# Engine orders found by single-move search and written out, in a fused block-sorted attention and gated SSM kernel

## Chip, cores and metric

One core of a Trainium2 chip. The metric is the device time in microseconds (us) of one execution. Lower is better. Each comparison runs both kernels in turn on the same chip. The granted clock is the share of full speed that the trace records for TensorE. Executions in which it is low or the time stands apart are marked slow; comparisons are made between fast runs.

Names used below: PE is TensorE, ACT ScalarE, DVE VectorE, POOL GpSimd, SP SyncE. The profile calls the instruction streams of SP and POOL "SPq" and "POOLq".

## The reference

Attention over sequences that are cut into 8 blocks of 96, where keys and values are first mixed across blocks by a matrix P (five Sinkhorn rounds of row and column normalisation), and then a gated layer with a linear scan over the sequence:

```python
batch, n_heads, seq, head_dim = (4, 8, 768, 64)          # 8 blocks of 96
# P: five rounds of exp, row and column normalisation of sort_net
k_sorted = einsum('bhij,bhjcd->bhicd', P, k_b)            # v_sorted alike
attn = softmax(scale * q_b @ k_sb.T)                      # per block
x = (attn @ v_sb) ...                                     # -> (4, 768, 512)
proj = x @ w_in                                           # 512 -> 1024
val, gate = proj[..., :512], proj[..., 512:]
h = a[0, 0] * h + val[:, t, :]; ys[:, t, :] = h           # scan over t
out = (silu(gate) * ys) @ w_out                           # 512 -> 512
```

## The kernel before

The kernel does not write its instructions down in order. It declares some 780 operations with what each reads and writes, its possible engines and an assumed cost, and a list scheduler in the same file turns them into one order per engine while the kernel is built. Semaphores keep these orders on the chip: each engine takes its operations as they are written, so one late operand stops everything behind it on that engine.

Names of operations (`b` is the batch, `h` the head, `p` the pair of heads, 4 pairs to a batch):

- `ld_QB`, `ld_KB`, `ld_VB`, `ld_wout`: loads from HBM, issued by POOL. POOL also does the gate multiplications `um`.
- `vs b_h` (PE) and `vse b_h` (ACT or DVE): sorted V of one head, and its copy from PSUM, the memory that PE writes its products to, into the buffer VSS.
- `vm b`: the **move** of a whole batch's sorted V from VSS to VA, which brings it to another set of partitions. It is 8 DMAs issued by SP, and needs all eight `vse` of its batch.
- `av p_k` (PE): attention times V, the first reader of VA. `rz`, `xn` (DVE, some ACT) normalise it, `xt` (PE) transposes it.
- `ks`, `kse`, `qt`, `qte`: sorted K and transposed Q with their copies. `pv`, `pg` (PE): projections. `o`, `oe`: outputs.

```python
HW_DMA = {"store": (2000.0, 7300.0, 780.0), "move": (3000.0, 6700.0, 2600.0), ...}   # ns
...
if o.kind in ("load", "fine"):
    dma_free = max(dma_free, t + cost) + o.dma / LOAD_RATES[o.kind == "fine"]
    ...
else:
    now = t + cost                          # SP has issued all pieces
    quick, slow, moved = HW_DMA[o.kind]
    if dma_free > now:                      # loads placed so far are still in flight
        o.end = now + slow
        ...                                 # and those loads are made later
    else:
        o.end = max(now, hw_free) + quick
```

So a move is booked at 5.1 us of issue plus 6.7 us if the load queue, by this reckoning, still has work at the instant SP is done, and at 5.1 plus 3.0 if it has none. The choice is made once, when the move is placed. Loads issued after that are never held against it.

The order itself came from priorities, with a correction for each operation in a long hexadecimal string (the scheduler's inner loop is cut here; the form of a matmul is the part of PE's array that it uses, `128*128` or `128*64` in the lines below; in the chain of the kernel before, 24 matmuls of the second form take 0.79 us behind the first and 0.67 behind their own):

```python
key = max(t, t_min) + pull * o.prio         # smallest key goes next on its engine
if e == "PE" and o.mode != mode:
    key += stick * ENTER[o.mode]            # a change of form counts against it
...
P.schedule(8, pull=5.859375, stick=0.1, nudge=NUDGE)
```

The softmax here doesn't subtract the row's maximum and nothing guards it: scores larger than these inputs give would overflow.

## Time and profile before

| | before |
|---|---|
| time, median of 3 runs | 123.95 us (123.77 to 125.11) |
| profiled span | 121.7 us |
| first sorted-K product / first projection / PE's end | 12.74 / 27.62 / 118.57 us |
| granted clock, whole span | 1.00 |

The 27.62 is where the view of the chain starts the first projection, and the prediction uses it. PE's timeline has it at 27.46, which is the figure to set beside the timelines of the other kernels.

This is SP's timeline of the kernel before, with start, length, engine, line and operation of the three moves:

```profile
28.55 5.22 SPq L671 DMA_DIRECT2D VA<-VSS  x8
49.82 5.90 SPq L671 DMA_DIRECT2D VA<-VSS  x8
69.52 5.07 SPq L671 DMA_DIRECT2D VA<-VSS  x8
```

And this is PE's timeline at the first readers of the first two moves. A bracket at a line's end gives the idle time before it and what ended it:

```profile
40.34 0.51 PE L733 MATMUL PSA<-VA,EX 96*128 96x65 bf16 x11
...
62.13 0.36 PE L733 MATMUL PSA<-VA,EX 96*128 96x65 bf16 x6 [0.22 <-DMA VA<-VSS]
```

From the start of SP's issue to the first use, 11.8 and 12.3 us pass. PE does not wait at the first, and waits 0.22 us at the second, so both moves are hidden with nearly nothing to spare. By the view of DMA issues, one piece of the first two moves takes 6.0 and 6.1 us to land, and one of the third, when loads are over, takes 2.8.

### The profile page before, as it was taken

The page shows a single profiled execution, that of the slowest core. Times are in us where ns is not written, and L with a number is a line of the kernel's source. Part 1 is how long each engine was busy: PE and PEld are TensorE (multiplying, and loading weights), DVE is VectorE, ACT ScalarE, POOL GpSimd, SP SyncE. Part 2 cuts the span into 40 slices and gives each one's busy share as a digit, 9 for nine tenths or more (in the row PEclk, how much of TensorE's full clock was granted, in tenths as well). Part 3 has the DMA queues.
Part 4 walks back from the last instruction along what each step waited for, and adds up shares of the span by engine and source line. Part 5 has one row for each costly group of instructions (what it writes and reads, how often), then busy time and mean ns, then how long its engine had stood idle before and what let it go on. Part 6 is the DMA issues. An engine that isn't in the chain of part 4 may idle for free.

```text
span 121.7 us, 3684 instructions
## 1 busy us (share of the span) xinstructions
PE 112.2 (92%) x1485; PEld 74.7 (61%) x1485; DVE 100.0 (82%) x239; ACT 84.0 (69%) x183; POOL 59.5 (49%) x84
## 2 busy tenths in 40 slices
PE   1689989999999999999999999999799999999990
PEld 1577778765766777667556586766466655554530
DVE  3774897999998999977599999999799999995300
ACT  4126879999868988898866977887634423365761
POOL 7999999999955620200028065000011396235500
PEclk9999999999999999999999999999999999999999
DMA  1999999999999999999999868289892000422665
GB/s 6 149 176 188 199 212 209 204 205 203 217 247 236 202 208 215 225 251 239 253 293 251 128 102 154 100 151 144 287 260 48 5 0 0 172 89 86 226 252 216
DMA packets 26305, 21.33 MB, mean 175 GB/s; under 512 B 7472, under 2 KB 22832, under 8 KB 26288
## 3 DMA queue, kind: packets, MB, share of 16 engines
q0 software_dynamic: 13824, 11.01, 58.3%
q1 hardware_dynamic: 12464, 10.08, 30.8%
q8 instruction: 12, 0.20, 0.6%
q14 instruction: 5, 0.04, 0.1%
HBM read 22.03 MB, written 6.29 MB: 233 GB/s over the span
## 4 chain that ended last, share of the span: by engine, by line
PE 66%; DMA 10%; DVE 9%; ACT 4%; SPq 4%; POOL 2%; issue 1%; POOLq 0%
PE PSA L800 31%; PE PSA L836 14%; DMA VA<-VSS 6%; PE PSA L733 5%; DVE XN L754 5%; DMA QB<-in_q_dram 4%; SPq L671 4%; PE PSA L703 4%; PE PSA L609 4%; PE PSA L625 3%; PE PSA L662 2%; ACT EX L713 2%; PE PSA L776 1%; DVE XT L417 1%; DVE RZ L745 1%
## 5 line engine op out<-in xcount | busy, mean ns | idle before, releaser
L819 POOL TENSOR_TENSOR GA<-GA,YS 128x384 bf16<-128x384 bf16 x30 | 27.2, 917 | 55.3 <-DVE GA L816 32.0
L800 PE MATMUL PSA<-XT,WIN 128*128 128x384 bf16 x256 | 45.4, 326 | 0.8 <-DVE XN L754 0.8
L800 PEld LDWEIGHTS PSA<-XT,WIN 128*128 128x128 bf16 x256 | 23.9, 98 | 16.3 <-DVE XN L754 0.9
L713 ACT ACTIVATE EX<-PSA 96x384 bf16<-96x384 f32 x64 | 26.3, 488 | 2.4 <-PE PSA L703 2.1
L813 ACT ACTIVATE TH<-PSA 128x384 f32<-128x384 f32 x32 | 15.7, 492 | 15.0 <-PE PSA L800 13.8
L836 PE MATMUL PSA<-WOUT,GA 128*128 128x512 bf16 (+1 forms) x100 | 23.2, 370 | 0.0
L754 DVE TENSOR_TENSOR XN<-PSA,RZ 96x320 bf16<-96x320 f32 (+2 forms) x49 | 21.7, 470 | 0.2
L816 DVE SCALAR_TENSOR_TENSOR GA<-TH,PSA 128x384 bf16<-128x384 f32 x32 | 17.0, 542 | 5.3 <-ACT TH L813 4.2
L415 ACT ACTIVATE OUTSB<-PSA 128x512 f32<-128x512 f32 (+1 forms) x23 | 13.4, 581 | 7.3 <-PE PSA L836 7.1
L807 DVE TENSOR_TENSOR_SCAN YS<-AEXP,YS,PSA 128x384 bf16<-128x384 f32 x16 | 15.7, 999 | 0.3 <-PE PSA L800 0.2
L807 DVE TENSOR_TENSOR_SCAN YS<-AEXP,PSA 128x384 bf16<-128x384 f32 x16 | 14.8, 940 | 0.7 <-PE PSA L800 0.7
L733 PE MATMUL PSA<-VA,EX 96*128 96x65 bf16 x256 | 13.7, 194 | 0.5 <-DVE XN L754 0.2
L836 PEld LDWEIGHTS PSA<-WOUT,GA 128*128 128x128 bf16 x100 | 9.0, 97 | 8.2 <-ACT OUTSB L415 0.3
L733 PEld LDWEIGHTS PSA<-VA,EX 96*128 96x128 bf16 x256 | 10.9, 98 | 4.7 <-DMA VA<-VSS 0.8
L745 DVE RECIPROCAL RZ<-PSA 96x5 f32<-96x5 f32 (+2 forms) x52 | 8.3, 175 | 2.0 <-PE PSA L733 1.6
L415 ACT ACTIVATE KTS<-PSA 128x768 bf16<-128x768 f32 x11 | 8.6, 811 | 1.4 <-PE PSA L625 1.3
L703 PE MATMUL PSA<-QTS,KTS 64*96 64x96 bf16 x256 | 9.5, 210 | 0.0
L703 PEld LDWEIGHTS PSA<-QTS,KTS 64*96 64x96 bf16 x256 | 7.2, 121 | 3.6 <-DVE KTS L417 0.4
L609 PE MATMUL PSA<-IDENT,QB 128*64 128x128 bf16 x192 | 7.8, 238 | 1.3 <-DMA QB<-in_q_dram 1.3
L415 ACT ACTIVATE VSS<-PSA 128x384 bf16<-128x384 f32 x19 | 8.4, 504 | 0.3 <-PE PSA L662 0.3
L625 PE MATMUL PSA<-LALL,KB 128*64 128x128 bf16 x192 | 7.4, 221 | 0.7 <-ACT EX L713 0.6
L427 POOL DMA_DIRECT2D QB<-in_q_dram x10 | 7.7, 782 | 0.3 <-issue 0.3
(60 smaller groups left out, 122.2 us busy)
## 6 DMA issues: line engine op xcount, KB each, us to landing
out_dram<-OUTSB SPq DMA_DIRECT2D x23, 256.0 KB, 2.5
VA<-VSS SPq DMA_DIRECT2D x24, 97.5 KB, 5.7
VB<-in_v_dram POOLq DMA_DIRECT2D x6, 384.0 KB, 20.1
KB<-in_k_dram POOLq DMA_DIRECT2D x6, 384.0 KB, 23.9
QB<-in_q_dram POOLq DMA_DIRECT2D x6, 384.0 KB, 21.5
WIN<-in_moe_w_in_dram POOLq DMA_DIRECT2D x1, 1024.0 KB, 11.1
QB<-in_q_dram POOLq DMA_DIRECT2D x4, 192.0 KB, 5.1
KB<-in_k_dram POOLq DMA_DIRECT2D x4, 192.0 KB, 6.1
```

What stands on the lines that cost most here:

```text
L415: return eng.activation(dst, src, AF.Copy, scale=1.0 if scale is None else scale)
L609: ins = e.transpose(PSB[u.bank][64 * x:64 * x + 64, t * 128:(t + 1) * 128], QB[sl][:, 2 * pr + x, t * 64:(t + 1) * 64], IDENT[:, :])
L703: ins = e.matmul(PS[us[half, x].bank][0:BLK, il * BLK:(il + 1) * BLK], KTS[ks][r, i * BLK:(i + 1) * BLK], qt(r, i))
L713: op("ex%d_%d_%d" % (p, half, x), act_cost(HALF), lambda e, n, u=us[half, x], es=es, half=half: e.activation(EX[es][:, half, 0:HALF].rearr ...
L733: ins = e.matmul(PS[u.bank][:, (kk - k0) * 65:(kk - k0 + 1) * 65], EX[es][:, i // 4, (i % 4) * BLK:(i % 4) * BLK + 128], VA[vs][:, i, hx * ...
L754: return e.tensor_tensor(XN[xs][:, k0 * D:(k0 + nb) * D].rearrange("p (n d) -> p n d", d=D), pv(u, nb)[:, :, 0:64], bass.AP(RZ[rz], 0, [[6 ...
L800: ins = e.matmul(PS[u.bank][:, 0:HALF], WIN[:, c, col:col + 128], XT[(4 * b + c) % NXT][:, half * HALF:(half + 1) * HALF], start=(c == 0), ...
L807: op("sc%d_%d_%d" % (b, ch, half), {"DVE": 65 + 384 * 2.1}, lambda e, n, u=u: e.tensor_tensor_scan(YS[slot][:, :], AEXP[:, ch:ch + 1].to_b ...
L813: op("th%d_%d_%d" % (b, ch, half), act_cost(HALF), lambda e, n, u=w: e.activation(TH[ts][:, :], PS[u.bank][:, 0:HALF], AF.Tanh, scale=0.5) ...
L816: op("ga%d_%d_%d" % (b, ch, half), dve_cost(HALF), lambda e, n, u=w: e.scalar_tensor_tensor(GA[slot][:, :], TH[ts][:, :], 1.0, PS[u.bank][ ...
L819: op("um%d_%d_%d" % (b, ch, half), {"POOL": 900, "DVE": 500} if b == B - 1 and half else {"POOL": 900}, lambda e, n: e.tensor_tensor(GA[sl ...
L836: ins = e.matmul(PS[u.bank][:, 0:c1 - c0], GA[slots[ch]][:, tl * 128:(tl + 1) * 128], WOUT[:, ch, c0:c1], start=(ch == 0), stop=(ch == 3))
```

## The change

Intent: take the order that the scheduler had found, improve it by trying single moves of operations (and of copies between ACT and DVE), each judged by a timetable of the same kind that keeps the order fixed and also counts loads that come late, and write the best orders into the kernel. No operation is added or removed. 18 copies go from ACT to DVE and 18 back. POOL now issues the last loads between gate multiplications instead of ahead of all of them.

```diff
-NUDGE = ("787d6199da75884466907dde6a737596fd557b9f2b38bd7a8772678d756e7c8d..." (cut)
+ORDER = (
+    "004f0050005100aa005200670053005400550056007b005700580059005a005c..."   # PE (cut)
+    ...                                                    # ACT, DVE, POOL, SP
+)
-    def schedule(self, n_banks, pull=0.0, stick=1.0, nudge=None):
+    def replay(self, n_banks, order):
+        todo = {e: [self.ops[int(x[i:i + 4], 16)] for i in range(0, len(x), 4)] for e, x in zip(engines, order)}
... (choice by priority removed; the earliest head of the five orders is placed next)
+                if at[e] == len(todo[e]) or todo[e][at[e]].left:
                     continue
+                o = todo[e][at[e]]
+                t = max(o.ready, free[e])
... (PSUM banks by the same rule as before; the branch on dma_free is unchanged)
-        P.schedule(8, pull=5.859375, stick=0.1, nudge=NUDGE)
+        P.replay(8, ORDER)
```

## The prediction

> **What bounds the kernel now.** I read the page's busy shares first, then its chain of work, TensorE's waits, the busy time in five stretches, and last the merged chain, for unit costs.
>
> ```profile
> PE 112.2 (92%) x1485; PEld 74.7 (61%) x1485; DVE 100.0 (82%) x239; ACT 84.0 (69%) x183; POOL 59.5 (49%) x84
> ...
> PE 66%; DMA 10%; DVE 9%; ACT 4%; SPq 4%; POOL 2%; issue 1%; POOLq 0%
> ```
>
> TensorE (PE) is busy 92% of the span of 121.7 us and is two thirds of the chain; VectorE (DVE) follows at 82%. All that TensorE waited for, in the whole run:
>
> ```profile
> PE PSA L539 <- ACT PSA L517: 2.7, 1, 2.7
> PE PSA L609 <- DMA QB<-in_q_dram: 1.3, 2, 0.9
> PE PSA L800 <- DVE XN L754: 0.8, 1, 0.8
> PE PSA L625 <- ACT EX L713: 0.6, 1, 0.6
> PE PSA L554 <- DVE PT L548: 0.3, 1, 0.3
> PE PSA L733 <- DVE XN L754: 0.2, 1, 0.2
> PE PSA L733 <- DMA VA<-VSS: 0.2, 1, 0.2
> ```
>
> The first is the start. The two waits for Q loads (1.3) fall before 9 us, where the Sinkhorn steps on DVE and ScalarE (ACT) set the pace to 10.9 us anyway. After that only 2.1 us of named waits are left. The stretches, cut at the first sorted-K product (12.74), the first projection (27.62), the first attention product of batch 2 (62.13), the last projections, and TensorE's end (118.57):
>
> ```profile
> 12.74:27.62 14.88, 13.79 (x289) 10.96 (x290) 13.65 (x41) 14.09 (x34) 14.85 (x26) 1.00 1.25 206
> 27.62:62.13 34.51, 34.29 (x525) 22.84 (x523) 30.16 (x64) 29.60 (x69) 12.96 (x16) 1.00 1.26 230
> 62.13:101.69 39.56, 38.80 (x477) 25.11 (x478) 38.06 (x85) 25.25 (x54) 13.50 (x15) 1.00 0.66 139
> ```
>
> Columns: length, then busy time of PE, PEld, DVE, ACT, POOL, the clock, the DMA share, GB/s. In the first stretch DVE and ACT are as full as PE: it is bound by emptying PSUM. In the second, PE never visibly stops. In the third DVE is nearly as full as PE (38.1 to 38.8 of 39.6). Transfers run at a share over 1 until about 67 us: the queue of input loads is full for half the run.
>
> **What is hidden in "busy".** Four neighbouring rows of the merged chain (start, duration):
>
> ```profile
> 31.98 0.79 PE PSA L625 x24
> 32.77 0.67 PE PSA L609 x24
> 33.45 0.67 PE PSA L625 x24
> 34.12 4.01 PE PSA L800 x24
> ```
>
> The same 24 column-half matmuls take 0.79 us when they come after a full-array matmul and 0.67 after their own kind; 24 projection matmuls after them take 4.01, where 24 x 0.1625 (20 take 3.25 elsewhere in the chain) is 3.90. So each change of array form costs about 0.115 us. Other unit costs, from start to start in the same view: projection group of 4, 0.65; output group of 4, 0.865; 16 score matmuls 0.37 plus the change; one attention-value matmul 0.031; 12 sorted or Q-transpose matmuls 0.335; one V-sort matmul 0.163; 8 transposes 0.345.
>
> [...]
>
> **How much could be won.** Units times counts, from 12.74 to 118.57. First stretch: work 10.2, 15 changes of form 1.7, together 11.9 of 14.88: 3.0 us lost. Second: work 31.8 (21 projection groups 13.65, 6 outputs 5.2, 16 sorted or Q sets 5.4, the rest 7.6), 21 changes 2.4, together 34.2 of 34.51: 0.3 lost. Third, to the end: work 53.7 (43 projection groups 28.0, 18 outputs 15.6, the rest 10.1), 14 changes 1.6, together 55.3 of 56.44: 1.1 lost, 0.76 of it the one wait for DVE at 85.6. In all 4.4 us lost and 5.8 us of changes. No operation is added or removed, so these are all that a new order can attack; start and tail (2.5 us of the last copy and store after PE's end) stay. 2% is 2.5 us: more than half of all losses.
>
> **The change part by part.** I decoded both orders into names of operations. Nothing but order, engine of some copies, and PSUM bank differs.
>
> 1. *Changes of form.* From the first sorted-K product on, PE changes form 50 times before and 45 after (the K and Q sets of batches 1 and 2 stand together). 5 x 0.115 = **-0.6 us**. Two more come at the start, beside Sinkhorn: nothing.
>
> 2. *Balance in the first stretch.* 18 copies go each way between ACT and DVE. In this stretch three normalisations of batch 0 leave ACT (4 x 0.22 = 0.87 each) and one comes; two half transposes leave and one comes (0.37 each); two V-sort copies come (0.40 each): ACT -1.75 - 0.37 + 0.8 = -1.3 us. DVE: +2 x 0.33 + 0.28 - 2 x 0.47 = 0. The two are full together, so at most half of 1.3 shortens the stretch; DVE stays full. I take **-0.4** (0 to -1.0).
>
> 3. *The wait at 85.6.* The first projection of batch 2 now stands before the attention products of the last heads, so DVE's backlog has them to hide it. **-0.6** of 0.76. The other small waits: -0.1.
>
> 4. *Start.* The identity (0.23) and the mask (0.38, of which 0.28 fits in a gap) now stand between Sinkhorn steps: +0.3 on their chain. But PE was 0.45 late for the product that follows it (10.93 to 11.38), and one Q set less now stands before it. Sum about **-0.1**.
>
> 5. *Later loads.* Before, all loads are issued by 33.3 us. Now the last ten or so stand behind gate multiplications on GpSimd, the last three behind those of the second half of batch 0, near 49 us by my estimate. The queue is some 15 us deep then, so its end moves little. But Q for batch 2 is wanted about 6 us sooner: the set that ran at 45 us follows, by the summed units, at about 39. Q's first part of batch 2 landed at 42.8 (issued 24.0 + 18.8); without the output weight ahead of it, and with loads that start 0.7 sooner, I estimate 39 to 40. Two of batch 1's V-sort copies are late on ACT, which puts the move of V (landing 5.7 us after issue) at about 42 where the order wants it at 41.5 to 42. The second V half of batch 2 lands near 49 where it is wanted at 48. Three tight meetings, each between 0 and 1.5 us of wait; the intent says that late loads were counted. I take **+0.6** in all.
>
> Sum: -0.6 - 0.4 - 0.6 - 0.1 - 0.1 + 0.6 = -1.2. From 123.95: **122.7 us**.
>
> **The rivals.** (a) *The loads bite.* PE waits at the three meetings of point 5 and the gains are eaten: 123.5 to 124.8. For it: PE takes orders strictly, so one late Q set stops everything behind it. Against: the stretch before them is bound by DVE and ACT too, so PE may arrive later than I sum. (b) *The order is as good as its aim*: half of the first stretch's 3.0 us and nearly all of the third's come free, no load is met: -0.6 - 1.5 - 1.0 = -3.1, 120.9. For it: every single move was tried. Against: DVE works 13.65 us in that stretch in any order, and gives none of its work up. (c) *ACT becomes the bound between 31 and 50 us*: DVE hands it net some 2.5 us of copies there (about 3.5 us on ACT, which is busy about 16.7 of 20). Then PE waits for banks, and point 1 is lost: 123.5. (d) *DVE stays the bound from 20 to 50 us* whatever PE's order: point 1 buys nothing before 62 us: 123.0.
>
> **Range and chances.** The middle is between rivals (d) and (b). Range 121.3 to 124.1 us: its low end is two thirds of what is lost, its high end is rival (a) half true. Faster by over 2% needs 121.5 or less; I give that 0.18, mostly (b). Slower by over 2% needs new waits of more than 3.5 us beyond the gains: 0.03. Within 2%: 0.79.
>
> **What would show it.** Right: span near 120.5; PE's busy sum about 0.5 us less; first projection near 27.2; no wait of PE for DVE's XN near 85; a few tenths of PE waiting for transfers (QB or VA) between 38 and 50. Step 1 is wrong if the time from first projection to PE's end, waits taken away, doesn't fall. Step 2 is wrong if the first projection starts before 26.5 or after 27.7. Step 5 is wrong if PE waits for transfers over 1.5 us, or not at all. The prediction as a whole is wrong if the first stretch gives over 1.5 us, or if loads issued behind GpSimd's multiplications let the queue run dry.

## More of the kernel before

The move, as declared, and its place in the scheduler's timetable:

```python
if pr == 3:
    def mv(e, n):
        return [e.dma_start(VA[va][:, i, :], VSS[vs][16 * i:16 * i + 16, :, :]) for i in range(NB)]
    op("vm%d" % b, {"SP": 8 * 640}, mv,
       reads=[("VSS", vs, x) for x in range(H)] + [...],
       writes=[("VA", va, x) for x in range(4)], dma=1160000, kind="move", parts=NB, prio=p - 4.8)
```

## The result

The changed kernel takes **131.12 us** (median of 4 runs, 129.75 to 133.24) against 123.86 (4 runs). The ratio of fast runs is 1.0525 (1.0402 to 1.0648): slower. The results are correct. (Ratios here are the mean time of one kernel's fast runs over that of the other's of the same rounds, so not quite the ratio of the medians.) Its profiled run was a slow one, 133.24 us with a span of 131.1. The other three have a clock of 0.979 to 0.986 in the mean, so part of what slows that run is in all of them. The trace below is of the slow run: its sums explain that run, and the fast runs (130.66 us in the mean) lost 6.5 us.

The page of the kernel after, with the clock in 40 slices of 3.28 us:

```profile
PE 114.7 (87%) x1485; PEld 75.6 (58%) x1485; DVE 99.9 (76%) x239; ACT 81.4 (62%) x177; POOL 59.6 (45%) x84
...
PEclk9999689999999756999999999999999999999998
...
PE 61%; DMA 15%; SPq 8%; ACT 5%; POOL 5%; DVE 2%; issue 1%; POOLq 0%
```

PE's share fell from 92 to 87% though it is busy 2.5 us longer, DMA and SP grew from 14 to 23% of the chain, and the clock has two dips (before it had none). The first, at a clock of 0.50 from 14 to 17 us, has no wait longer than 0.82 us in the ten us before it; whether the fast runs have it too is not on record. What PE waited for:

```profile
PE PSA L682 <- DMA VA<-VSS: 5.3, 2, 2.8
PE PSA L488 <- DVE IDENT L427: 3.6, 1, 3.6
PE PSA L558 <- DMA QB<-in_q_dram: 0.8, 1, 0.8
...
PE PSA L749 <- ACT EX L662: 0.7, 1, 0.7
PE PSA L574 <- DMA KB<-in_k_dram: 0.4, 1, 0.4
```

The second is the start, which costs nothing new. The first is new: 5.3 us in two waits, both for a move of V. Line 682 is `av` (733 before). PE's timeline around the two, start and length first:

```profile
41.81 0.81 PE L749 MATMUL PSA<-XT,WIN 128*128 128x384 bf16 x4
45.41 0.49 PE L682 MATMUL PSA<-VA,EX 96*128 96x65 bf16 x6 [2.79 <-DMA VA<-VSS]
45.71 1.47 PE L749 MATMUL PSA<-XT,WIN 128*128 128x384 bf16 x4
...
52.29 0.81 PE L749 MATMUL PSA<-XT,WIN 128*128 128x384 bf16 x4
...
69.16 0.35 PE L682 MATMUL PSA<-VA,EX 96*128 96x65 bf16 x6 [2.49 <-DMA VA<-VSS]
```

Four projection matmuls take 0.81 us at 41.81, 1.47 right after the first wait, and 0.81 again at 52.29: **after the wait PE ran at about half speed** for 6.5 us. The busy time by stretch says it too (length; PE, PEld, DVE, ACT, POOL; clock; DMA share; GB/s):

```profile
27.89:45.41 17.52, 14.67 (x235) 9.97 (x232) 12.60 (x22) 12.76 (x29) 9.91 (x12) 0.98 1.26 214
45.41:51.90 6.49, 6.49 (x49) 3.75 (x50) 4.06 (x12) 2.54 (x5) 2.55 (x3) 0.54 1.31 203
51.90:69.16 17.26, 14.77 (x231) 9.82 (x229) 12.07 (x25) 13.72 (x29) 4.06 (x5) 1.00 1.15 225
```

A stretch of 6.49 us at a clock of 0.54 holds 3.5 us of full-speed work, so 3.0 us are lost there without any wait being listed. PE counts as fully busy in it: this loss is invisible in the shares, and only the clock shows it.

PE ends at 126.79, 8.2 us later than before. That is: first projection 0.4 later (27.89 for 27.46), waits for moves 5.3, half clock 3.0, the rest 0.5 better. The end of the span came another 1.2 us later after the last copy out of PSUM (3.7 for 2.5). There the stores are issued closer together, five in 3.9 us; that this is the reason was not tested.

Why are the moves late? SP's timeline after, and the two rows of the chain where the last pieces land (start and length):

```profile
33.17 6.28 SPq L620 DMA_DIRECT2D VA<-VSS  x8
57.22 6.20 SPq L620 DMA_DIRECT2D VA<-VSS  x8
77.95 5.86 SPq L620 DMA_DIRECT2D VA<-VSS  x8
```

```profile
38.83 6.45 DMA VA<-VSS
...
62.81 6.22 DMA VA<-VSS
```

The first move runs from 33.17 to 45.28, 12.1 us, and PE stood before its reader at 45.41 - 2.79 = 42.62: the order gives it 9.45. The second runs from 57.22 to 69.03, 11.8 us, and again gets 9.45. Set beside what the kernel's own timetable, computed when it is built, books for each move (end of issue plus quick or slow landing):

| | chip: issue to landing | timetable: start -> end (length) | first reader in the timetable |
|---|---|---|---|
| before, 1st | about 11.2 (5.22 + one piece 6.0) | 27.84 -> 39.66 (11.8) | 39.73 |
| before, 2nd | 12.3 (49.82 to 55.12 + 6.97) | 49.25 -> 61.07 (11.8) | 61.15 |
| before, 3rd | about 7.9 (5.07 + 2.8) | 68.56 -> 76.68 (8.1) | |
| after, 1st | **12.1** | 31.81 -> 39.93 (**8.1**) | 40.94 |
| after, 2nd | **11.8** | 50.11 -> 58.23 (**8.1**) | 59.23 |
| after, 3rd | about 8.8 (5.86 + 2.9) | 68.07 -> 76.19 (8.1) | |

Both lengths in the timetable are good: 11.8 beside loads, 8.1 without. What is wrong is which of them the new order gets. For its first two moves it books 8.1 while the chip takes 12. The overrun less the margin of 1.0 us that the timetable left gives 12.1 - 8.1 - 1.0 = 3.0 and 11.8 - 8.1 - 1.0 = 2.7 us of wait; measured are 2.79 and 2.49.

The reason is the branch on `dma_free`. In the new order GpSimd holds loads back behind gate multiplications, and `ld_wout` starts at 32.72 in the timetable, after the move's 31.81, so it doesn't count. For the second move the last load placed before it leaves the queue at 55.14 by the timetable, and SP is done at 55.23. A difference of 0.09 us decides for 8.1, and one more load (starting at 50.55) is not looked at since it comes later. On the chip loads are in flight at both moves. In the stretch from 27.89 to 45.41 the share of busy DMA is 1.26. At the second move the queue had nearly run out (share 0.66 and 47 GB/s from 58 to 59 us), but the last three loads, which the timetable starts at 49.1 to 50.5, were issued at 56.30 to 58.60, around the move's start at 57.22, and from 60 to 61 us the share is 1.31 again.

By its own timetable the new order ends at 119.23 against 119.99: 0.76 us better. The theory to be tested is therefore: **the search found a way to have its moves booked as quick, and the chip doesn't honour it**; the moves are started later (33.17 for 28.55) and come late, and PE's half clock after the wait adds to it. That the search was led by this branch is not seen in any trace; the timetable itself is asked at the end. Rivals: the loads that are held back cause the loss by themselves; or PE's new order or the new balance of copies is slow for another reason.

### The profile page after: what moved, and what is told of

Same layout as the page of the kernel before. It is cut to its first block, busy times and chain, and to the rows that moved or that the text cites.

```text
span 131.1 us, 3668 instructions
## 1 busy us (share of the span) xinstructions
PE 114.7 (87%) x1485; PEld 75.6 (58%) x1485; DVE 99.9 (76%) x239; ACT 81.4 (62%) x177; POOL 59.6 (45%) x84
## 4 chain that ended last, share of the span: by engine, by line
PE 61%; DMA 15%; SPq 8%; ACT 5%; POOL 5%; DVE 2%; issue 1%; POOLq 0%
PE PSA L749 26%; PE PSA L785 14%; DMA VA<-VSS 10%; SPq L620 8%; PE PSA L682 7%; DMA KB<-in_k_dram 5%; PE PSA L652 4%; PE PSA L574 3%; PE PSA L611 3%; POOL QB L376 2%; PE PSA L596 2%; PE PSA L725 1%; ACT OUTSB L364 1%; ACT VSS L364 1%; POOL KB L376 1%
## 5 line engine op out<-in xcount | busy, mean ns | idle before, releaser
L749 PE MATMUL PSA<-XT,WIN 128*128 128x384 bf16 x256 | 47.1, 329 | 0.7 <-ACT EX L662 0.7
L785 PE MATMUL PSA<-WOUT,GA 128*128 128x512 bf16 (+1 forms) x100 | 24.9, 386 | 0.0
L703 DVE TENSOR_TENSOR XN<-PSA,RZ 96x320 bf16<-96x320 f32 (+2 forms) x51 | 22.7, 471 | 0.5
L682 PEld LDWEIGHTS PSA<-VA,EX 96*128 96x128 bf16 x256 | 11.7, 102 | 10.0 <-issue 6.5
L364 ACT ACTIVATE OUTSB<-PSA 128x512 f32<-128x512 f32 (+1 forms) x20 | 11.4, 582 | 5.8 <-PE PSA L785 5.7
L364 ACT ACTIVATE VSS<-PSA 128x384 bf16<-128x384 f32 x21 | 9.7, 530 | 5.1 <-PE PSA L611 3.2
L364 ACT ACTIVATE KTS<-PSA 128x768 bf16<-128x768 f32 x13 | 10.0, 815 | 0.2 <-PE PSA L574 0.2
L574 PE MATMUL PSA<-LALL,KB 128*64 128x128 bf16 x192 | 7.9, 226 | 0.4 <-DMA KB<-in_k_dram 0.4
```

The lines of the kernel that those rows point to most:

```text
L364: return eng.activation(dst, src, AF.Copy, scale=1.0 if scale is None else scale)
L574: ins = e.matmul(PSA[64 * x:64 * x + 64, c0:c0 + 128], buf[sl][:, h, t * 64:(t + 1) * 64], lm(b * H + h))
L682: ins = e.matmul(PS[u.bank][:, (kk - k0) * 65:(kk - k0 + 1) * 65], EX[es][:, i // 4, (i % 4) * BLK:(i % 4) * BLK + 128], VA[vs][:, i, hx * ...
L703: return e.tensor_tensor(XN[xs][:, k0 * D:(k0 + nb) * D].rearrange("p (n d) -> p n d", d=D), pv(u, nb)[:, :, 0:64], bass.AP(RZ[rz], 0, [[6 ...
L749: ins = e.matmul(PS[u.bank][:, 0:HALF], WIN[:, c, col:col + 128], XT[(4 * b + c) % NXT][:, half * HALF:(half + 1) * HALF], start=(c == 0), ...
L785: ins = e.matmul(PS[u.bank][:, 0:c1 - c0], GA[slots[ch]][:, tl * 128:(tl + 1) * 128], WOUT[:, ch, c0:c1], start=(ch == 0), stop=(ch == 3))
```

## The experiments

Fourteen kernels ran. Edits are given by operation names in the written-out orders. Lines of the experimental kernels stand 4 below those of the changed kernel (`av` is L686), since the table of orders is printed with four more lines. All gave correct results.

**e8, a control.** The order of the kernel before, written out in the new form.

```diff
-ORDER = (new orders)
+ORDER = (each engine's order as the scheduler before gives it)
```

> Control: the kernel before with its own orders written out, the same instructions, waits and banks. Ratio to the kernel before 1.000, within 0.005. Its profile shows whether the late start of TensorE (first sorted-K product at 14.0 to 14.2 us instead of 12.7) seen in two profiles of the first four runs, one of which has the start of the kernel before, comes with the run: then it may appear here too.

Measured: 124.1 us (12 runs), ratio 0.9994 (0.996 to 1.0028). The form of the kernel costs nothing; all of the loss is in the orders.

**e2: the old kernel with only the first move late.** Every load stays early.

```diff
 # order of the kernel before, ACT
-... ex3_1_0 vse1_2 vse1_1 vse1_0 vse1_3 ...
+... ex3_1_0 vse1_2 vse1_3 ...
-... xte2_4 th0_3_0 kse4 ...
+... xte2_4 th0_3_0 vse1_1 vse1_0 kse4 ...
```

> The kernel before, its orders written out (same program, instruction for instruction), with the one thing done to it: the same two V-sort copies of batch 1 put off on ScalarE until behind the tanh of the first projections. Theory 1: the move is issued about 4.4 us later, near 33, and lands near 45, TensorE waits about 4 us before the attention-value products of batch 1, then runs at half clock for some us; the time is 5 to 8 us longer than before, and the load order had nothing to do with it. Rival (load order): within 1 us of before, as all loads are still issued by 33 us.

Measured: 130.46 us, ratio 1.0537 (1.045 to 1.0624). SP's timeline, then PE's waits:

```profile
34.41 5.76 SPq L624 DMA_DIRECT2D VA<-VSS  x8
```

```profile
PE PSA L686 <- DMA VA<-VSS: 3.4, 1, 3.4
```

The clock is 0.64 from 48 to 52 us. Two copies of 0.5 us each, run later on ACT, cost the old kernel as much as the whole change costs. In this profile the start was 1.2 us late as well, which some profiles show and others of nearly the same start do not (below), so not all of its 6.7 us (by the ratio) need belong to the move.

**e1: the changed kernel with only the first move early.**

```diff
 # ACT
-... vse1_5 th0_0_0 xte1_4 th0_2_0 xte3_4 vse1_1 th0_1_0 vse1_0 th0_3_0 ...
+... vse1_5 vse1_1 vse1_0 th0_0_0 xte1_4 th0_2_0 xte3_4 th0_1_0 th0_3_0 ...
```

> The changed kernel with one edit on ScalarE: the copies of the last two V-sort results of batch 1 (heads 1 and 0) stand right behind the other six instead of among the tanh and transpose copies that follow. Theory 1 (the order gives the move of V from its trigger to its first use 9.5 us, where it takes 12 us while loads are in flight): the first move is issued near 29 us instead of 33.2 and lands near 41, TensorE's wait of 2.8 us before the first attention-value products of batch 1 goes, and with it the stretch at half clock behind it (45.4 to 51.9); the second wait (2.5 us, batch 2) stays. Span near 125, time 4 to 6 us below the changed kernel. Rival (loads issued late behind GpSimd's multiplications make the move slow): the wait of 2 us or more stays, as no load is moved.

Measured: 129.12 us (129.01 to 129.25), ratio 1.039 (1.035 to 1.043), clock 0.992 to 1.0. SP's timeline, then PE's waits:

```profile
29.51 5.44 SPq L624 DMA_DIRECT2D VA<-VSS  x8
```

```profile
PE PSA L686 <- DMA VA<-VSS: 2.9, 1, 2.9
PE PSA L562 <- DMA QB<-in_q_dram: 2.1, 3, 1.0
```

The first wait and the dip behind it are gone, and the second wait stays, as the second move has not been touched. But by the ratios only 1.7 us came back, where 4 to 6 were expected. A wait of 1.0 us for Q now stands at 41.6. It is not one that the late V had hidden: PE's order has these Q products ahead of the first reader of VA, and e4 shows both waits (0.92 us for Q that ends at 40.0, then 2.04 us for V). The first stretch also began 1.6 us late in this profile, and with it the issue of that load (26.29 for 24.46).

**e4: the rival of the loads.** All loads ahead of the first gate multiplication, in their new sequence; nothing else.

```diff
 # POOL
-... um0_0_0 ld_... um0_... ld_KB3_4 um0_0_1 um0_3_1 ld_VB3_4 ld_QB3_4 ld_QB3_0 um1_1_1 ...
+... (all ld_, lmat24) um0_0_0 um0_... um1_1_1 ...
```

> The changed kernel with all loads on GpSimd ahead of its first gate multiplication, in their own order, as it was before the change (they stood behind multiplications from the output weight on). Theory 1: the first wait stays within 1 us of its 2.8, since the move runs beside loads in either case; the second move may gain, as the last three loads no longer start together with it, 0 to 2.5 us. Time 0 to 3 us below the changed kernel. Rival (late loads slow the move and are the cause): both waits go and the time comes to within 1 us of the kernel before.

Measured: 130.6 us, ratio 1.0513 (1.0424 to 1.0602). The waits for moves are 2.04 and 1.78 us, and the clock is 0.61 from 44 to 48. The loads held back are not the cause by themselves: with all of them early, nearly the whole loss remains. The expected gain of up to 3 us did not come either.

**e3 and e12: idle matmuls in the waits.** They give no work, and are meant to keep the clock up. e3 puts 50 ahead of `av5_0` (first wait), e12 also 46 ahead of `av9_0` (second). The edit of e12:

```diff
+        def fill_op(name, n_mm):
+            uf = Unit(name)
+            def fill_mm(e, n):
+                for i in range(n_mm):
+                    ins = e.matmul(PS[uf.bank][:, 0:128], IDENT[:, :], IDENT[:, :])
+                return ins
+            op(name, {"PE": 54 * n_mm}, fill_mm, reads=["IDENT"], writes=[uf], units=[uf])
+        fill_op("fill1", 50); fill_op("fill2", 46)
         P.replay(8, ORDER)
```

> The changed kernel with 50 matmuls of 128 columns into a PSUM bank of their own, whose result nobody reads, put on TensorE just before the first attention-value products of batch 1 (2.7 us of work in the wait of 2.8 us). If the half clock in 45.4 to 51.9 comes from the wait, it goes: the granted clock is 1.0 there, the move lands at the same time near 45.3, and the time falls by about 3 us (6.5 us at clock 0.54 hold about 3.5 us of work). If the clock falls for another reason, the time is the same or longer.

e3 measured: 130.58 us, ratio 1.050 (1.0452 to 1.0547). A miss. The clock is 1.0 from 44 to 52, as hoped, but the dip came back after the second wait, which in the changed kernel had none. The busy time of e3 from 66 to 70 us:

```profile
66.00:70.00 4.00, 3.90 (x32) 2.42 (x33) 1.62 (x3) 1.67 (x4) 0.00 (x0) 0.57 0.55 182
```

So whether a wait of this length is followed by half clock depends on more than its length. Waits of 2.79 us (changed kernel), 2.04 (e4), 2.5 (e3) and 3.6 (e7, below) were followed by a clock of 0.57, 0.61, 0.57 and 0.58 over 4 us; the wait of 2.49 us that ends at 69.16 in the changed kernel and one of 2.86 us in e1 by 1.00. In e11 (below), behind two waits of 0.52 and 0.53 us, the last of which ends at 26.73, a V-sort matmul took 0.52 us at 29.19, where it took 0.34 at 26.73. What decides it these runs don't show.

> The changed kernel with idle matmuls in both waits for the moves (50 before the attention-value products of batch 1, 46 before those of batch 2). The moves land when they did, so the waits themselves (5.3 us) are not shortened; if the half clock after a wait is a cost of its own, the granted clock is 1.0 in every stretch from 20 us on and the time is 1.5 to 3 us below the changed kernel (127.5 to 129); with one wait filled the dip had only moved to the second (clock 0.57 at 66 to 70 us).

e12 measured: 128.36 us (fast runs 128.16 to 128.42), ratio 1.0301 (1.024 to 1.0363). Its clock, in 40 slices:

```profile
PEclk9999999999999999999999999999999999999999
```

With both waits filled the clock stays up. Means of fast runs: 130.66 for the changed kernel, 128.3 here, so the half clock costs 2.3 us of the 6.5 (2.8 by the two ratios). The waits are still there in substance, filled with idle work (2.96 us at 42.03, 2.73 at 63.45).

**e5, e6: both moves early.** e5 is e1 with the second move early too: the second half of V ahead of Q on POOL, and the `vs2` and `vse2` operations sooner on PE, ACT and DVE. e6 also puts the first half of Q of batch 2 ahead of V.

```diff
 # e5: POOL
-... ld_QB2_4 ... ld_VB2_4 ...
+... ld_VB2_4 ld_QB2_4 ...
 # e5: PE
-... av6_6 o2 av6_0 vs2_1 vs2_0 pv0_0_1 ... vs2_7 vs2_5 vs2_6 ... vs2_4 xt5_0 ...
+... av6_6 vs2_1 vs2_0 vs2_7 vs2_5 vs2_6 vs2_4 o2 av6_0 pv0_0_1 ... xt5_0 ...
 # e5: the same for their copies, ACT behind qte8, DVE behind xn4_11
 # e6: POOL as well
+... ld_QB2_0 ld_VB2_0 ...
```

> The run with the first move early, and the second move's trigger brought forward as well: the load of V for heads 4 to 7 of batch 2 is issued ahead of those of Q and K for the same heads, its four V-sort products stand some 3 us sooner on TensorE, and their copies sooner on ScalarE and VectorE. Theory 1 (order gives the second move 9.5 us where it takes 12): the trigger comes about 3 us sooner, the gap from trigger to first use becomes 12 us or more, the wait of 2.9 us at the first attention-value products of batch 2 falls below 0.5, and the time falls by 2 to 3 us against the run with the first move early (129.1 to about 126.5). Rival (the moves are only slow because of how loads and moves collide, whatever the gap): the wait stays above 1.5 us.

> As the run with both moves early, and the first Q load of batch 2 issued ahead of the first V load of batch 2. The 1 us that TensorE waits near 41 us for Q of batch 2 goes (the load lands about 2 us sooner); time 0.5 to 1 us below the run with both moves early.

e5 measured: 127.84 us, ratio 1.0304 (1.0238 to 1.037), clock 1.0: 1.1 us below e1 by the ratios, where 2 to 3 were expected. The second move starts at 50.65, and no wait for a move is left. What stands in their place are waits for loads: 0.89 us for K at 36.4, 1.02 for Q at 41.5, 0.8 for V of batch 3 at 65.2.

e6 measured: 129.24 us, ratio 1.0454 (1.0373 to 1.0535), with two of its four runs marked slow. The ratio can't be had without those two: the mean of the fast ones (127.16 and 128.81) is 1.031 times that of the fast runs of the kernel before. So e6 is level with e5, and the expected 0.5 to 1 us did not come. The wait for Q is gone, and V of batch 3, one of the loads held behind gate multiplications, is waited for longer:

```profile
PE PSA L615 <- DMA VB<-in_v_dram: 2.6, 1, 2.6
```

These V products stand behind the first reader of the second move in PE's order. So the late loads do cost time, as I had predicted, but it shows only when the late second move no longer covers it.

**e9: the loads early as well.** e6 with all loads ahead of the gate multiplications, and V of batch 3 ahead of its K and Q.

```diff
 # POOL, behind the loads of batch 1 and the first Q and V of batch 2
+ld_wout ld_VB2_4 ld_QB2_4 ld_KB2_4 lmat24 ld_KB2_0 ld_VB3_0 ld_VB3_4 ld_KB3_0 ld_KB3_4 ld_QB3_4 ld_QB3_0 um0_0_0 um0_... 
```

> The changed kernel with both moves early (as in the run of that name), the first Q load of batch 2 ahead of the first V load, and all loads on GpSimd ahead of its first gate multiplication, those of batch 3's V before its K and Q. Theory 1 completed (behind the waits for the moves stood waits for the loads that are held back: 0.8 to 3.6 us for V of batch 3 in the last three runs): with both repaired no wait of TensorE for a move or a load over 1 us is left after the first projection, and the time comes to within 1 us of the kernel before (123.5 to 125). If a third cause in the new order remains, the time stays above 126.

Measured: 125.26 us (20 runs, 124.49 to 126.41) against 124.43 (42 runs), ratio 1.0074 (1.0046 to 1.0101). PE's waits of e9, of which the first is the start:

```profile
PE PSA L492 <- DVE IDENT L431: 3.6, 1, 3.6
PE PSA L578 <- DMA KB<-in_k_dram: 1.3, 1, 1.3
PE PSA L498 <- DVE PBF L482: 0.6, 1, 0.6
```

The expectation was met in part: a wait of over 1 us for a load is left, and 125.26 is just above its 125. Of the 6.5 us, 5.6 come back (1.0525 to 1.0074) by edits that only make transfers start sooner: the loads, and the V-sort products and copies ahead of the moves. The rest of the new orders is kept. This is the main evidence for the theory, with an addition: early moves alone (e5) bring back 2.7 us, early loads alone (e4) 0.1, both together 5.6, with intervals of 0.3 (e9) to 1.5 us (changed kernel) each way. The late moves and the late loads cover each other.

**e14: a quiet second move.** The direct test of what makes a move long. The changed kernel, with its last three loads made to wait for `av9_0`, so that only the end of one earlier load (it lands at 58.3) is in flight during the second move. It is bound to be slow, since the loads then come late.

```diff
+        by = {x.name: x for x in P.ops}
+        for name in ("ld_VB3_4", "ld_QB3_4", "ld_QB3_0"):
+            by[name].deps[by["av9_0"]] = 1
         P.replay(8, ORDER)
```

> The changed kernel with the last three loads (V, Q, Q of batch 3) made to wait until the first use of the second move. If loads beside it make a move long, the pieces of the second move land about 3 us after issue instead of 6.2, the move takes 8 to 9.5 us instead of 11.8, and TensorE's wait at the first attention-value products of batch 2 falls from 2.5 us to below 1; a new wait for V of batch 3 comes instead, so the time may be longer. If the move's length has nothing to do with the loads, its pieces still land after 6 us and the wait stays.

Measured: 136.61 us (134.11 to 138.77, no ratio formed). SP's timeline, then PE's waits:

```profile
55.79 5.42 SPq L624 DMA_DIRECT2D VA<-VSS  x8
```

```profile
PE PSA L615 <- DMA VB<-in_v_dram: 5.1, 1, 5.1
...
PE PSA L686 <- DMA VA<-VSS: 2.5, 1, 2.5
```

The view of DMA issues has the eight pieces of the second move, first in the changed kernel, then here (KB of one piece, us from issue to landing):

```profile
VA<-VSS SPq DMA_DIRECT2D x8, 97.5 KB, 6.2
```

```profile
VA<-VSS SPq DMA_DIRECT2D x8, 97.5 KB, 2.9
```

So the move takes about 8.3 us here. The one wait for a move that is left, 2.5 us, is the first one's; at `av9_0` there is none. The timetable's 8.1 is right when loads are (nearly) out of the way, and loads in flight are what adds the missing 3.5 us. In the traces of before, after, e1, e2, e5, e9 and e14 the median piece of a move lands in 2.8 to 2.9 us with no loads of GpSimd in flight or only the end of one, and in 5.7 to 6.5 us beside them.

**e7, e10, e11, e13: is there anything in the new order worth keeping?** e7 is e6 with the old start on all engines. e10 is the kernel before with one copy taken from DVE's backlog to ACT. e11 is the kernel before with the changed kernel's first stretch (12.6 to 27.9 us), V early, and that copy. e13 is e9 with the K products of pairs 6 and 7 later, behind the load that e9 waits for.

```diff
 # e10, from the kernel before
-DVE: ... sc1_2_1 kse13 rz8_6 ...      ACT: ... kse12 oe6 ...
+DVE: ... sc1_2_1 rz8_6 ...            ACT: ... kse12 kse13 oe6 ...
 # e13, from e9: PE (and kse6 kse7 behind ex5_0_0 on ACT)
-... qt6 ks6 ks7 pv0_1_1 st5_0 pg0_1_1 pv0_3_1 ...
+... qt6 pv0_1_1 st5_0 pg0_1_1 ks6 ks7 pv0_3_1 ...
```

> As the run before it, and the order of the kernel before on every engine up to the first sorted-K product (identity and mask ahead of the Sinkhorn steps, the iota first on GpSimd, loads of Q, K and V mixed, Q products in pairs). If the start cost something, the first sorted-K product comes sooner and the time falls by 0.3 to 1.5 us, to near that of the kernel before (124 to 125); if the start is a matter of the run and not of the order, within 0.5 us of the run before it.

> The kernel before with one copy (sorted K of pair 13) given from VectorE to ScalarE. VectorE's backlog before the first projections of batch 2 is 0.95 us shorter, so TensorE's wait of 0.76 us for a PSUM bank there shrinks to 0 to 0.3; time 0.3 to 0.8 us below the kernel before, if that wait was on the path; else the same within 0.2 us.

> The kernel before with two things: that copy given to ScalarE, and the new order's first stretch (from the first sorted-K product to the first projection, on TensorE, ScalarE and VectorE, with the two V-sort copies early); all loads, moves and the rest as before. If the new order's gain in that stretch is real (14.2 to 15.0 us against 14.7 to 15.3), the time is 0.3 to 0.8 us below that of the run before it, and the version is faster than both kernels: 122.5 to 123.5. If not, as the run before it.

> As the run with both moves early and the loads first, and the two sorted-K products of batch 1 that waited 1.3 us for their load stand behind one more projection pair and a score set on TensorE (two more changes of array form), their copies likewise on ScalarE. If the wait was on the path, it goes and the time falls by 0.7 to 1.2 us, to 124.0 to 124.6: level with the kernel before (ratio 0.995 to 1.003). If the new order held a gain of its own of the size I had predicted (1.2 us), the ratio is below 0.993.

| | median us | ratio | what it showed |
|---|---|---|---|
| e7 | 130.26 | 1.048 (1.0411 to 1.055) | first K product at 12.71 instead of 12.64: the old start is no better; the wait for V of batch 3 grew to 3.6, with a dip (clock 0.58 from 66 to 70 us). Miss |
| e10 | 125.04 (22 runs) | 1.0025 (0.9994 to 1.0057) | PE still waits 0.8 us for XN: that copy was not its cause. Miss |
| e11 | 128.06 | 1.0262 (1.0206 to 1.0319) | the grafted stretch took 16.8 us, with PE slower at its end (a V-sort matmul took 0.52 us at 29.19, for 0.34 at 26.73). Miss |
| e13 | 125.71 | 1.0131 (1.0073 to 1.0188) | the wait for K fell from 1.3 to 0.5, one of 0.5 for a copy came; no gain. Miss |

No version beat the kernel before. In the profiles of e1, e2 and e11 the first stretch began 1.2 to 1.6 us late, in others of nearly the same start not. I could not tie this to an edit; it stays open.

## Why the prediction was wrong

I predicted 122.7 us (121.3 to 124.1) and gave 0.03 to what happened. The step that failed is the fifth: it had the length of the moves under load and the cost of waiting for them wrong. By its own steps:

1. **Fewer changes of form, -0.6: not found.** By the test I had set (from first projection to PE's end, waits taken away) nothing fell: 118.57 - 27.46 = 91.1 before, 90.1 without its waits of 0.76 and 0.22; in e9, the version without waits for moves and without a dip behind them, 119.57 - 27.21 = 92.4, 90.8 without its waits of 1.29 and 0.23. Why five changes of form fewer, at about 0.115 us each in the chain of the kernel before, buy nothing was not settled.
2. **First stretch, -0.4: not shown.** The new order's first projection starts at 26.9 to 27.9 in e3, e4, e5, e6, e9, e12, e13 and e14 (27.5 in the middle), the old one's at 27.5 to 27.7 in the kernel before, e8 and e10. In the changed kernel's profile (27.89, outside the 26.5 to 27.7 that I had set) a clock dip (0.50 from 14 to 17 us) lies in this stretch, and in that of e11 PE is slower at its end.
3. **The wait at 85.6, -0.6: gone, but not free in the changed kernel.** That one waits 0.65 us at 94.3, for an exponential of ACT this time. In e9 the wait there is 0.23, for a transfer. e10 shows that relieving DVE of one copy doesn't remove it in the old order.
4. **Start, -0.1: not shown.** First sorted-K product at 12.63 for 12.74, as forecast; but the old order has it at 12.31 in e8 and 12.30 in e10, so the match is luck.
5. **Later loads, +0.6: the step that failed.** I had seen the first meeting ("puts the move of V (landing 5.7 us after issue) at about 42 where the order wants it at 41.5 to 42"), and sized it 0 to 1.5 us. The move was triggered at 33.17, where my 42 stood for about 31, and took 12.1 us, where I took 5.2 + 5.7 = 10.9; it landed at 45.3, and PE wanted it at 42.6. For the second move I checked only the load of its V, not the move itself: another 2.5 us. And I counted a wait as its own length alone: the half clock behind it cost 2.3 to 3.0 us more. As a sum, with the waits of the slow profiled run: 2.8 + 2.5 + 2.3 to 3.0 = 7.6 to 8.3 instead of 0.6. My own sign for this step was waits for transfers over 1.5 us; they were 5.3. And the last three loads, which I put near 49 us, were issued from 56.3; the load queue did nearly run dry at 58, a sign I had named for the whole. It cost nothing there by itself: PE worked without a wait from 51.90 to 66.67.

The median of 5.7 us for a piece was a mixture: 6.0 and 6.1 for the moves beside loads, 2.8 for the one after them. The gap from trigger to first use in the kernel before, 11.8 and 12.3 us with a wait of 0.2, was in the trace and said directly that a move needs 12. My sentence "the intent says that late loads were counted" was trust in the timetable where its branch should have been read.

Rival (a), "the loads bite", had the right direction and named the right reason (one late operand stops PE, for 2.79 and 2.49 us here), at 123.5 to 124.8, because it too counted three small waits. Rivals (b) and (c) didn't occur. The outcome of (d), that point 1 buys nothing, came; its reason did not show, as PE's waits for DVE after the first projection are 0.2 us in e9. "Start and tail stay" was off by 1.2 us at the tail, and the tail before is 3.1 us from PE's end (121.7 - 118.57): the 2.5 count from the end of the last copy. That loads issued by GpSimd make pieces issued by SP land later is shown by e14 (6.2 us beside them, 2.9 without).

On the gain of the search itself: 0.76 us by the timetable. It is of the size of the timetable's errors, and the search, which keeps whatever lowers the computed end, kept two moves booked 4 us too short. That the branch is what the search exploited is an inference from the timetable (the 0.09 us, the load that starts 0.9 us after the move). It can be made firmer without the chip, by computing the timetable again. With the branch forced to the slow landing for the first two moves, the new order ends at 124.74 instead of 119.23, which is 4.75 us behind the old order. e4's order, in which the early loads make the timetable book both moves at 11.8, ends at 124.74 too, while on the chip e4 and the changed kernel take the same time (130.6 and 131.12 us). So the new order is better than the old only with the quick booking. The 4.75 and the half clock of 2.3 make 7.1 us, an estimate near the 6.5 lost. That late transfers are where the time went, the moves first and the loads behind them, is shown by e2, e5, e9 and e14; e1 shows it for the first wait.

## What to carry to other kernels

When a search writes an order from a cost model, look first at what the model decides by a single comparison, and compare the trigger-to-first-use gap of every hidden transfer in the new order with its measured length under the same load: here 9.45 us were given to something that the old trace already showed to take 12. Count a wait of TensorE as more than its length where its trace shows a lower clock behind it: here the half clock behind one cost 2.3 to 3.0 us more, while behind waits of 2.49 and 2.86 us the clock stayed at 1.00. And when one late transfer is mended, expect the next one to show: the late second move had hidden the late load of V of batch 3 (0.8 us of wait in e5, 2.6 in e6).
